# A re-annealed order of the steps of attention, routing and the first expert, under a list scheduler

## The chip, the cores and the metric

The kernel runs on one core of one Trainium2 chip. Times are device microseconds (us) of that core. A run is called fast or slow by the rules of the measurement; every run here counted as fast, but the mean granted TensorE clock of single runs still differs (0.994 to 1.000). The engines are PE (matmul; PEld is its weight load), DVE (vector), ACT (scalar), POOL (GpSimd) and SP (which issues transfers).

## The reference, cut to what matters

```python
def phi(x):                                   # attention features, of q and of k
    proj = einsum('bhsd,df->bhsf', x, w_phi)
    proj = proj - max(abs(proj), axis=-1)
    return concatenate([exp(proj), exp(-proj)], axis=-1)
# 8 batches, 8 heads, 576 rows, 64 columns; 128 features, twice
num, den = q_p @ (k_p.T @ v), q_p @ sum(k_p)  # x = num / den, as [4608, 512]
P = exp(x @ w_gate)                           # routing: 8 rounds of row and column scaling
for e in range(8):                            # eight experts, all of them on all rows
    out += P[:, e:e+1] * (relu(x @ w1[e]) @ w2[e])
```

The routing needs all of x (its column sums run over all 4608 rows). So attention has to end before the routing can start. The first expert's two products need no routing weights until they are scaled, so they serve as filling material for PE during attention and during the routing.

## The kernel before

The program is written as a list of small operations with a modelled duration each. A list scheduler turns the list into one fixed instruction order per engine:

```python
    def schedule(self):
        ...
            best = None
            for eng, rq in ready.items():
                ...
                for o in rq:
                    t = self.start(o, f)
                    if t is not None and (best is None or (t, o.idx) < best[:2]):
                        best = (t, o.idx, o)      # earliest start, then written order
        ...
            if o.nbytes:                          # a transfer: one server for all of them
                dma_free = max(at + o.dur + 1.0, dma_free) + o.nbytes / 1e3
                o.end = dma_free + 1.0
```

What is changed is the written order of the steps:

```python
    STEPS = {"a": stage_a, "q": lambda i: qs[i](), "r": stage_r, "b": stage_b,
             "c": lambda j: pair_c(j // 4, j % 4, xbs[j]), "g": stage_g,
             "u": lambda i: up0(i // 4, i % 4), "d": lambda i: down0(i // 4, i % 4)}
    order = ("aqraqabbcqabqacbqrbcaqbacuqaqbacqruabgqccucbudbduaqabdqadgrcbucqucabqcauqdua" ...)
    for i, n in enumerate(order):
        STEPS[n](order[:i].count(n))
    gate(8)
    ...
    routing()
    for i in fill:                                # the rest of the first expert
        expert0(i)
```

The letters: a takes a pair of heads (keys, scores, maxima, exponentials) and issues the loads of the next batch; q does the same for queries; r is the rest rows; b the products of attention; c the transposition into xT; g the logits; u and d are each one of 36 steps of the first expert's up and down product (8 matmuls of 512 columns in a step). A step a also issues a transposing transfer of what was loaded:

```python
            load_qk(b + 1, 2 * pr, 4, t, gt)      # POOL queue: two loads with a cast
            load_v(b + 1, 2 * pr, 4, t, gt)       # SP queue
            if b + 1 >= 2:
                turn_qk(t)                        # SP queue: dma_start_transpose, qkT<-qk
        ...
            load_w0(n, gt)                        # POOL queue: a piece of the first expert
```

After P exists, the first expert's results are scaled by it on ACT, while PE goes on with the second expert:

```python
        if e == 1 and g < 9:
            for ts in range(4):
                act(512, lambda ts=ts: nc.scalar.activation(
                    out=acc[g][:, ts, :], in_=acc[g][:, ts, :], func=ACT.Copy, bias=0.0,
                    scale=P[:, 4 * g + ts, 0:1]), ["P", ("acc", g, ts)] + akey(g), ...)
```

Of the kernel before, what the change touches and what calls it, by code (L numbers as in the profile page):

```python
# [168 lines left out]
def kernel(  # L169
# [636 lines left out]
    def stage_g(b):  # L806
# [5 lines left out]
             "c": lambda j: pair_c(j // 4, j % 4, xbs[j]), "g": stage_g,  # L812
             "u": lambda i: up0(i // 4, i % 4), "d": lambda i: down0(i // 4, i % 4)}
    order = (
        "aqraqabbcqabqacbqrbcaqbacuqaqbacqruabgqccucbudbduaqabdqadgrcbucqucabqcauqdua"
        "bgcbqaducdcqubcrbaudqauqdacbcdqduardqbbgcubuaqcaubgcdqacdqabubruqadbqadcbqbu"
        "cagcquaubqrdbadqaudbcqcaucbdcccqbgcg"
    )
    for i, n in enumerate(order):
        STEPS[n](order[:i].count(n))  # L820
# [456 lines left out]
```

## Time and profile before

| Kernel before | us |
|---|---|
| time, median of 3 runs | 1044.51 |
| span of the profiled run | 1043.5 |
| routing starts (attention is over) | 220.9 |
| P is written | 257.2 |
| PE alone carries the chain from | 298.2 |

The table of windows of the kernel before, three stretches of it. Columns: the stretch, its length, then busy us of each engine with the number of its instructions, the granted clock, the DMA share and GB/s.

```profile
core 0: us, PE busy (x) PEld busy (x) DVE busy (x) ACT busy (x) POOL busy (x), PEclk, DMA share, GB/s
50.00:75.00 25.00, 22.83 (x281) 15.07 (x280) 24.16 (x61) 24.00 (x66) 19.49 (x39) 1.00 1.32 196
75.00:100.00 25.00, 25.00 (x251) 15.63 (x251) 23.34 (x57) 23.84 (x62) 15.78 (x31) 1.00 0.89 156
225.00:250.00 25.00, 25.00 (x124) 12.09 (x123) 21.66 (x60) 10.35 (x18) 0.00 (x0) 1.00 0.49 179
```

In attention three engines are nearly full at once. In the routing (225 to 250 us) PE and DVE are, and ACT is not.

The two moments that divide the kernel, from the views of the two source lines: the routing's first reduce and the last instruction of P (duration in ns as smallest, median and largest, then the start in us of the first and the last such instruction).

```profile
L873 DVE TENSOR_REDUCE rr<-L x1: 444/444/444, 220.9 to 220.9; 128x36 f32<-128x288 f32 x1
L886 DVE TENSOR_TENSOR P<-T,c_bc x1: 457/457/457, 257.2 to 257.2; 128x288 f32<-128x288 f32 x1
```

The chain of work that ended last, in order of time (start, length, what):

```profile
218.43 38.47 PE P L407 x216
...
257.66 3.17 ACT acc L1181 x5
...
298.23 733.88 PE P L1019 x6720
```

PE fills the routing with first-expert matmuls (38.47 us), ACT's scalings follow P, and from 298 us on PE streams without a break.

Waits between 25 and 218 us, the ones of ACT and DVE for PE (who waited for whom, total us, times, longest):

```profile
DVE kv L587 <- PE P L407: 4.8, 5, 1.8
ACT hT L699 <- PE P L407: 3.7, 8, 1.2
ACT q L403 <- PE P L606: 3.6, 7, 0.8
DVE rec L624 <- PE P L611: 3.5, 9, 0.6
```

### The profile page before, as it was taken

How to read it: one execution, taken by the hardware profiler on the slowest of the kernel's cores; microseconds unless marked ns; L12 is line 12 of the kernel's file. 1: busy time of each engine (PE TensorE's matmuls, PEld its weight loads, DVE VectorE, ACT ScalarE, POOL GpSimd, SP SyncE). 2: the span in 40 equal slices, each digit the busy share in tenths (PEclk: the TensorE clock that was granted, in tenths of full speed). 3: DMA queues.
4: the chain of work that ended last, by engine and by line, in shares of the span. 5: the costliest groups of instructions: out<-in, count | busy, mean ns of one | idle time of the engine just before them, and what ended most of it. 6: DMA issues, size and time to landing. Idle time of an engine off the chain costs nothing.

```text
span 1043.5 us, 24529 instructions
## 1 busy us (share of the span) xinstructions
PE 1020.4 (98%) x9512; PEld 842.1 (81%) x9512; DVE 823.9 (79%) x1626; ACT 711.1 (68%) x1570; POOL 461.5 (44%) x532
## 2 busy tenths in 40 slices
PE   6899999999999999999999999999999999999998
PEld 4566666654788888888888888888888888888886
DVE  6999899998777787778877787778777877787775
ACT  7999999944976666666666666565666666666663
POOL 3876757500233344344444444444444443333442
PEclk9999999999999999999999999999999999999999
DMA  9997987734411152113311441134111611114333
GB/s 250 150 196 132 150 127 136 122 122 120 93 41 41 52 105 60 51 42 82 81 41 42 87 87 51 42 69 95 41 42 50 125 51 42 41 43 131 122 122 122
DMA packets 105237, 93.94 MB, mean 90 GB/s; under 512 B 45344, under 2 KB 80288, under 8 KB 105120
## 3 DMA queue, kind: packets, MB, share of 16 engines
q1 hardware_dynamic: 71840, 68.45, 23.6%
q0 software_dynamic: 33120, 23.86, 16.4%
q8 instruction: 74, 1.21, 0.5%
q14 instruction: 43, 0.35, 0.1%
q10 hardware_dynamic: 160, 0.07, 0.0%
HBM read 94.98 MB, written 14.16 MB: 105 GB/s over the span
## 4 chain that ended last, share of the span: by engine, by line
PE 89%; ACT 5%; DVE 3%; DMA 1%; issue 1%; SPq 0%; POOL 0%; DVEq 0%; ACTq 0%
PE P L1019 70%; PE P L407 16%; ACT acc L1181 2%; DVE m L399 1%; PE P L606 1%; ACT k L403 1%; DMA acc<-in_q_dram 1%; DMA wgate_f<-in_moe_w_gate_dram 1%; ACT V L1171 1%; ACT U L1047 1%; PE P L645 1%; DVE xb L626 0%; ACT q L403 0%; DVE P L618 0%; PE P L484 0%
## 5 line engine op out<-in xcount | busy, mean ns | idle before, releaser
L1174 POOL TENSOR_TENSOR acc<-acc,V 128x512 f32<-128x512 f32 x248 | 316.4, 1283 | 440.4 <-ACT V L1171 437.2
L1051 DVE CUSTOM_DVE_ANT_0 hT<-P,U 128x512 bf16<-128x512 f32 x378 | 255.0, 687 | 107.9 <-ACT U L1047 59.7
L1047 ACT COPY U<-P 128x512 f32<-128x512 f32 x378 | 217.8, 590 | 137.4 <-PE P L1019 130.8
L1171 ACT ACTIVATE V<-P,P 128x256 f32<-128x256 f32 x496 | 206.3, 477 | 123.4 <-PE P L1019 121.6
L1159 DVE SCALAR_TENSOR_TENSOR acc<-P,P,acc 128x256 f32<-128x256 f32 x372 | 160.1, 478 | 73.4 <-PE P L1019 71.7
L1019 PEld LDWEIGHTS <-w 128*128 128x128 bf16 x2016 | 197.3, 98 | 23.7 <-issue 0.6
L1019 PEld LDWEIGHTS <-S 128*128 128x128 bf16 x1984 | 194.1, 98 | 23.2 <-issue 0.6
L1019 PEld LDWEIGHTS <-T 128*128 128x128 bf16 x1512 | 147.9, 98 | 19.1 <-issue 2.0
L1019 PEld LDWEIGHTS <-hT 128*128 128x128 bf16 x1488 | 145.4, 98 | 18.3 <-DVE hT L1051 1.1
L1019 PE MATMUL P<-X,w 128*128 128x256 bf16 x1008 | 154.7, 273 | 0.4 <-ACT U L1047 0.4
L1019 PE MATMUL P<-xT,w 128*128 128x256 bf16 x1008 | 152.0, 273 | 0.0
L1019 PE MATMUL P<-X,T 128*128 128x256 bf16 x1008 | 148.6, 273 | 1.3 <-ACT U L1047 1.2
L1019 PE MATMUL P<-w,hT 128*128 128x256 bf16 x992 | 142.6, 273 | 0.6 <-DVE hT L1051 0.6
L1019 PE MATMUL P<-T,S 128*128 128x256 bf16 x1056 | 136.3, 273 | 0.4 <-ACT V L1171 0.4
L1019 PE MATMUL P<-w,S 128*128 128x256 bf16 x928 | 126.6, 273 | 0.0
L532 POOL TENSOR_TENSOR v<-v_m,em 128x512 bf16<-128x512 f32 x64 | 66.8, 1043 | 70.6 <-ACT em L403 57.5
L399 DVE TENSOR_REDUCE m<-P 128x4 f32<-128x512 f32 x128 | 82.7, 681 | 1.7 <-PE P L407 1.2
L1056 ACT ACTIVATE hT<-P 128x512 bf16<-128x512 f32 x126 | 74.6, 607 | 12.9 <-PE P L1019 12.4
L407 PE MATMUL P<-w,hT 128*128 128x512 bf16 x320 | 80.2, 379 | 0.3
L927 DVE TENSOR_TENSOR S<-hT 128x1024 bf16<-128x1024 bf16 x124 | 80.1, 683 | 0.0
L407 PE MATMUL P<-xT,w 128*128 128x512 bf16 x288 | 76.2, 379 | 1.2 <-ACT kr L403 0.5
L1019 PE MATMUL P<-xT,T 128*128 128x256 bf16 x504 | 76.3, 273 | 0.0
(94 smaller groups left out, 1091.7 us busy)
## 6 DMA issues: line engine op xcount, KB each, us to landing
X<-xd SPq DMA_DIRECT2D x126, 256.0 KB, 2.6
w<-in_moe_w_dram POOLq DMA_DIRECT2D x14, 1024.0 KB, 10.4
v_m<-in_v_dram SPq DMA_DIRECT2D x15, 512.0 KB, 5.1
out_dram<-acc SPq DMA_DIRECT2D x14, 512.0 KB, 3.2
xd<-S SPq DMA_DIRECT2D x18, 256.0 KB, 2.0
qk<-in_k_dram POOLq DMA_DIRECT2D x12, 256.0 KB, 5.5
qk<-in_q_dram POOLq DMA_DIRECT2D x12, 256.0 KB, 6.4
w<-in_moe_w_dram POOLq DMA_DIRECT2D x8, 256.0 KB, 7.5
```

Source lines behind the costliest of these rows:

```text
L399: dve(el, lambda: nc.vector.tensor_reduce(out=dst(), in_=src(), axis=AX.X, op=ALU.max, apply_absolute_value=True), r, w)
L407: nc.tensor.matmul(out_, lhsT=lhsT, rhs=rhs, start=start, stop=stop)
L532: pool(512, lambda y=y, em=em: nc.gpsimd.tensor_tensor(out=s["v"][y]()[:, :, 0:D], in0=t["v"]()[:, h0:h0 + 2].rearrange("p a (b c) -> p (a ...
L927: lambda: f.tensor_tensor(out=out_(), in0=x(), in1=y(), op=op), r, w, **kw)
L1019: pe(256, lambda i=i, k=k, z=z: nc.tensor.matmul(bank()[:, 256 * i:256 * i + 256], lhsT=lhs(k, i), rhs=rhs(k), start=first and z, stop=k = ...
L1047: act(512, lambda: nc.scalar.copy(out=u[fp][n]().rearrange("p a b -> p (a b)"), in_=x[fp]()), [x[fp]], [u[fp][n]])
L1051: dve(500, lambda: nc.vector._custom_dve(ADD_SAT, out=out_(fp, i, j), in0=bank[fp]().rearrange("p (a b) -> p a b", a=2), in1=u[fp][n](), s ...
L1056: act(512, lambda: nc.scalar.activation(out=out_(fp, i, j), in_=x[fp]().rearrange("p (a b) -> p a b", a=2), func=ACT.Relu, bias=0.0, scale ...
L1159: dve(330, lambda n=n, ts=ts: nc.vector.scalar_tensor_tensor(out=acc[g][:, ts, 256 * j:256 * j + 256], in0=bank()[:, 256 * n:256 * n + 256 ...
L1171: act(390, lambda n=n: nc.scalar.activation(out=u()[:, n, :], in_=bank()[:, 256 * n:256 * n + 256], func=ACT.Copy, bias=0.0, scale=P[:, 4 ...
L1174: pool(670, lambda: nc.gpsimd.tensor_tensor(out=acc[g][:, 2 * i:2 * i + 2, 256 * j:256 * j + 256], in0=acc[g][:, 2 * i:2 * i + 2, 256 * j: ...
L1181: act(512, lambda ts=ts: nc.scalar.activation(out=acc[g][:, ts, :], in_=acc[g][:, ts, :], func=ACT.Copy, bias=0.0, scale=P[:, 4 * g + ts, ...
```

## The change

Its intent: the written order is the priority of the list schedule. A search by annealing on the model of that schedule found another string with the same letters.

```diff
     order = (
-        "aqraqabbcqabqacbqrbcaqbacuqaqbacqruabgqccucbudbduaqabdqadgrcbucqucabqcauqdua"
-        "bgcbqaducdcqubcrbaudqauqdacbcdqduardqbbgcubuaqcaubgcdqacdqabubruqadbqadcbqbu"
-        "cagcquaubqrdbadqaudbcqcaucbdcccqbgcg"
+        "raqaqbabqacqaqbbrarccqbcabugucqabuqacqbcauqabbqcbadcruuuqbccaaqqbcbraddqugag"
+        "qbbdauqdbucaqrcccauaqbdccbuqgudabqadbdqdbcccrauqdaugdbcquaduqbaqcabudbcrqdaq"
+        "ccadbbuguqbadauuqcdbcuccaqudqbcbgcdg"
     )
```

## The prediction

> What bounds it now. (1) Attention, 0 to about 218 us. The table of windows gives, for 25 to 200 us (175 us), DVE 160 us busy, ACT 165, PE 167. No engine is the bottleneck alone: the waits from 25 to 218 us leave only 13.9 us idle on DVE and 12.8 us on ACT. [...] I count PE by issue steps in the trace (0.216 us for a 512-column matmul, 0.109 us for 256 columns, about 0.03 us for 65): an estimate of 186 us of PE stream in 218 us. About 32 us of PE time is empty, some 12 us of it in the first 25 us, where the chain of waits runs through the first loads (acc from q 6.7 us, w_gate 6.4 us). (2) Routing, 218.6 to 257.6 us: a DVE chain of eight iterations of about 5 us; PE is filled meanwhile with first-expert work (one piece of 38.5 us in the chain). (3) After P exists, ACT is full from 257.7 to 298 us (36 scalings of acc, 25.0 us, plus U, V, hT). From 298 us to the end PE streams at its rate (918 matmuls per 100 us); the change cannot touch that.
>
> What the change does. It permutes one string of 188 letters: 32 each of a, q, b, c, 24 u, 20 d, 8 r, 8 g in both. No instruction is added or removed; busy time per engine should be the same within 1 us. The string only sets priority among ready operations, the buffer turn, and the place of the gates on loads. The new string starts with r (whose loads land only at about 10 us, so the scheduler still starts with a), and holds the d steps back (7 instead of 11 after 108 letters, equal near the end).
>
> What it can gain. Only idle of the joint bottlenecks before 218 us. With 13 us idle on ACT and DVE, both waiting mostly for PE (hT 3.7, q 4.8, kv 4.8, rec 3.5 us), I expect a better order to recover 3 to 5 us, minus a loss because the model's durations are not the chip's. All of a shift of the end of attention should pass to the end: routing and the ACT stage start earlier by as much, and PE has about 5 us of slack in the ACT stage (an estimated 35 us of stream in 40 us) to take a backlog.
>
> Prediction: attention ends near 214.5 us, P near 254 us, the PE-bound stage starts near 294.5 us, and the total falls by 3.5 us to 1041.0 us; range 1035.5 to 1046.0. Faster by over 2%: 0.02 (21 us would need nearly all the early idle of every engine); within 2%: 0.96; slower by over 2%: 0.02.
>
> What would show it. Right: same instruction counts; the routing's first reduce and P earlier by 2 to 6 us; waits of ACT and DVE for PE between 25 and 218 us less by about as much; unchanged length of routing (37 us), ACT stage (40 us) and the stream after it (745 us). Wrong: attention's end earlier but routing longer, because more deferred first-expert work shares PE and DVE with it; or the ACT stage longer because PE comes with a backlog.
>
> What would make it wrong: a load gated later by the new place of a or q, so that a transpose starts late; turns of the eight PSUM buffers that the model orders otherwise than the chip; or an order fitted so closely to the model's durations that real ones break it, which could cost a few us.

## More of the kernel before

```profile
L407 PEld LDWEIGHTS <-w 128*128 128x128 bf16 x220 | 19.3, 98 | 14.6 <-issue 1.8 <-DVE xb L626 0.3
L407 PEld LDWEIGHTS <-hT 128*128 128x128 bf16 x168 | 15.0, 98 | 11.0 <-issue 0.7
...
L407 PEld LDWEIGHTS <-hT 128*128 128x128 bf16 x25 | 2.5, 98 | 2.9
```

Of the first expert's 576 matmuls, 388 are done when attention ends, and 25 are still owed when P exists.

## The result, and the profile after

| | before | after |
|---|---|---|
| time, median | 1044.92 us (4 runs) | 1046.20 us (4 runs, 1045.06 to 1047.42) |
| ratio | | 1.001 (95%: 0.9996 to 1.0024) |
| routing starts, profiled run | 220.9 | 219.6 |
| P begins, profiled run | 257.2 | 255.7 |
| span, profiled run | 1043.5 | 1045.1 |

Ratios are the mean time of one kernel's fast runs over that of the other's of the same rounds, so they are not quite the ratio of the medians quoted. The two kernels are equal within the measurement. The forecast gain of 3.5 us did not come. (The median of 1046.2 us is also 0.2 us above the top of the stated range; the ratio applied to the 1044.51 us of before gives 1045.6 us, inside it.)

The profile after, the same two lines:

```profile
L873 DVE TENSOR_REDUCE rr<-L x1: 447/447/447, 219.6 to 219.6; 128x36 f32<-128x288 f32 x1
L886 DVE TENSOR_TENSOR P<-T,c_bc x1: 459/459/459, 255.7 to 255.7; 128x288 f32<-128x288 f32 x1
```

P comes 1.5 us earlier, yet the span is 1.6 us longer. So something after P became 3.1 us longer, and something before it ate part of the gain. The first-expert weight loads, again up to the start of the routing and after P:

```profile
L407 PEld LDWEIGHTS <-w 128*128 128x128 bf16 x206 | 18.1, 98 | 12.3 <-issue 0.9
L407 PEld LDWEIGHTS <-hT 128*128 128x128 bf16 x167 | 14.9, 99 | 9.6 <-issue 0.5
...
L407 PEld LDWEIGHTS <-hT 128*128 128x128 bf16 x40 | 3.9, 98 | 4.7
L407 PEld LDWEIGHTS <-w 128*128 128x128 bf16 x1 | 0.1, 98 | 0.1
```

The new order has done 373 of the matmuls when attention ends, 15 fewer than the old one, and owes 41 when P exists, 16 more. At 0.216 us each (a run of eight takes 1.73 us in the chain of waits) that is 3.2 us of work not done in attention, and 3.5 us of work left for after P.

The chain that ended last, after:

```profile
61.10 14.54 DMA qkT<-qk
...
279.42 9.82 PE P L1019 x86
289.28 744.44 PE P L1019 x6817
```

Two things are new in it. From P to 279 us the chain still goes over ACT, but PE carries it from 279 us instead of 298: from there on PE is the late one now, not ACT. And there is a transposing transfer of 14.54 us. Around its landing the table of windows shows, after:

```profile
70.00:72.00 2.00, 2.00 (x22) 1.17 (x22) 1.70 (x5) 2.00 (x7) 1.66 (x5) 1.00 1.29 161
72.00:74.00 2.00, 0.66 (x19) 0.53 (x15) 1.54 (x6) 0.82 (x2) 0.00 (x0) 1.00 1.33 166
74.00:76.00 2.00, 0.31 (x3) 0.29 (x4) 0.00 (x0) 0.00 (x0) 0.00 (x0) 1.00 1.38 66
76.00:78.00 2.00, 1.78 (x18) 1.20 (x18) 1.44 (x3) 1.82 (x4) 1.56 (x2) 0.73 1.08 231
78.00:80.00 2.00, 2.00 (x17) 1.18 (x17) 1.63 (x4) 1.90 (x6) 0.00 (x0) 0.50 1.04 274
```

and before, for comparison, the third of these five stretches (PE is busy throughout all five there):

```profile
74.00:76.00 2.00, 2.00 (x14) 0.93 (x12) 2.00 (x6) 2.00 (x5) 0.40 (x2) 1.00 1.07 174
```

PE stands still from 72.7 us, all engines from 73.5 to 75.6 us. Then the granted clock falls to a half for some 3.4 us (it is 0.91 from 80 to 82 us). The lost clock is (0.27 + 0.50) x 2 = 1.5 us in the two rows shown. PE's own waits between 60 and 80 us name the reason:

```profile
PE P L407 <- DMA qkT<-qk: 3.0, 1, 3.0
```

The half clock follows the stall: here it comes after a wait of 3.0 us between matmuls. In the tables of windows of four later profiles, t_first (longest wait of PE around the stall 3.2 us; granted clock 0.55, 0.50, 0.50 and 0.74 in the four rows from 68 to 76 us) and early_rest_after (3.2 us; 0.70, 0.50 and 0.95 from 74 to 80 us) show the dip too, and after_again (0.8 us) and warm (2.0 us) stay at 1.00. From what length on a wait lowers the clock is not shown. A long wait is not the only way in: in the profile of hold1_before (below) the mean granted clock is 0.84 from 200 to 222 us, with PE busy for 17.45 of these 22 us, though its longest wait listed between 180 and 225 us is 0.8 us.

The waits that the prediction named did shrink: kv 4.8 to 3.2 us, hT 3.7 to 2.2, q 3.6 to 2.3, rec 3.5 to 3.0, together 4.9 us. But these four are a selection: over all waits of ACT and DVE for PE between 25 and 218 us the sum is 24.0 us in both profiles, because the stall brings new ones (ACT's `k` waits 4.6 us for PE instead of 1.5). In the profile of after_again (below), where PE waits only 0.8 us for the transposition, the sum is 19.1 us (25 to 214 us). So the new order does save waits, as it was made to, but only where the stall does not take them back.

### The profile page after: what moved, and what is told of

The parts are those of the page before. It is cut to its first block, busy times and chain, and to the rows that moved or that the text cites. A ratio compares the mean times of both kernels' runs of the same rounds, so it can differ in the third digit from the quotient of the medians.

```text
span 1045.1 us, 24505 instructions
## 1 busy us (share of the span) xinstructions
PE 1017.6 (97%) x9474; PEld 842.4 (81%) x9512; DVE 826.5 (79%) x1626; ACT 711.2 (68%) x1570; POOL 460.4 (44%) x532
## 4 chain that ended last, share of the span: by engine, by line
PE 91%; DMA 3%; DVE 2%; ACT 2%; issue 1%; SPq 0%; DVEq 0%; ACTq 0%
PE P L1019 72%; PE P L407 16%; DMA qkT<-qk 1%; PE P L606 1%; ACT acc L1181 1%; DVE m L399 1%; DMA acc<-in_k_dram 1%; DMA acc<-in_q_dram 1%; PE P L645 1%; DVE xb L626 0%; PE P L484 0%; ACT U L1047 0%; PE P L611 0%; SPq L329 0%; ACT acc L734 0%
## 5 line engine op out<-in xcount | busy, mean ns | idle before, releaser
L927 DVE TENSOR_TENSOR S<-hT 128x1024 bf16<-128x1024 bf16 x124 | 83.3, 709 | 0.0
L403 ACT ACTIVATE q<-P 128x512 bf16<-128x512 f32 x128 | 71.7, 629 | 4.0 <-PE P L606 2.7
```

The lines of the kernel that those rows point to most:

```text
L403: act(el, lambda: nc.scalar.activation(out=dst(), in_=src(), func=ACT.Exp, bias=0.0, scale=scale), r, w)
L927: lambda: f.tensor_tensor(out=out_(), in0=x(), in1=y(), op=op), r, w, **kw)
```

## The experiments

Two theories at the start. A: the gain of the new order is real and one stall, on the late transposition, eats it. B: the gain was never real; small waits everywhere eat it. The first group of runs led to a third, C: the order moves first-expert work from before P to after it, and the end pays for it. All experiments but hold1_before keep the fixed order of PE, ACT and DVE of the kernel that they start from; some repeat an instruction in it or add matmuls.

### The kernel after, once more, and its runs by clock

> The kernel after, unchanged, as the base of this group. Both theories: 1.000 to 1.002 of before. The four earlier runs fall in two groups by the mean granted clock: 0.997 to 0.998 with 1046.9 and 1047.4 us, 0.999 with 1045.1 and 1045.5 us. If the clock dip after the stall at 72.7 us comes and goes, these five runs show both groups again, about 1.7 us apart.

Six runs: 1043.79, 1048.08, 1044.43, 1043.81, 1048.22 and 1043.08 us, median 1044.12; ratio to before 1.0001 (0.9983 to 1.0018). With the four earlier ones there are ten. The four with a mean clock of 0.998 or less lie at 1046.88 to 1048.22 us (mean 1047.65), the six others at 1043.08 to 1045.51 us (mean 1044.28). So there are two groups, 3.4 us apart, which is more than the 1.7 us expected: it seems that the stall itself comes and goes, not only the clock. The profile of this kernel fell on a run without the dip (clock 1.000, 1043.79 us):

```profile
L873 DVE TENSOR_REDUCE rr<-L x1: 446/446/446, 216.4 to 216.4; 128x36 f32<-128x288 f32 x1
L886 DVE TENSOR_TENSOR P<-T,c_bc x1: 457/457/457, 252.5 to 252.5; 128x288 f32<-128x288 f32 x1
```

Undisturbed, the new order ends attention 4.5 us earlier than the old one, and P 4.7 us earlier: even more than I had forecast. But its span is 1042.0 us, only 1.5 us shorter. This is the main finding: 3.2 us are given back after P even where PE hardly stalls.

"Undisturbed" does not mean that the transposition was quick here. It took 14.3 us in this profile too, but it was issued at 59.4 us instead of 61.1, landed at 73.7, and PE waited 0.8 us for it instead of 3.0. The same DVE instructions of the two profiles start within 0.6 us of each other from 19 us until the stall. Right after it (`kv`, 74.6 against 76.6 us) the disturbed run is 1.9 us behind, at the end of the half clock (`rec`, 77.6 against 80.3 us) 2.8 us, and 3.1 us from 83 us on until the routing. In this pair of profiles, then, the stall makes about 1.9 us of the difference and the half clock 0.8 us.

### The transposition first

```diff
         done = self.schedule()
+        late = [done[n] for n in (844, 856, 877, 893)]   # k, q of the next half; two pieces of w2
+        for o in late:
+            done.remove(o)
+        n = done.index(self.ops[864]) + 1                # four POOL instructions later
+        done[n:n] = late
```

> The kernel after, with one thing moved: the four loads of GpSimd's queue (k and q of the next half batch, two pieces of w2) that start at 59.3 to 61.7 us, beside the transposing DMA of 61.1 us, are issued four GpSimd instructions later, so the transposition comes first. PE, ACT and DVE keep their order exactly. Theory A (the new order's gain is eaten by one stall: 3.0 us of all engines idle until the transposition lands at 75.6 us, then 1.7 us lost to a clock of a half): the transposition lands before 73 us, the stall shrinks under 1 us, no clock dip, and the time falls by 3 to 5 us against the kernel after, to 1041 to 1043 us. Theory B (the model's gain was never real; small waits all along the attention stage eat it): the stall shrinks, but the time stays within 1 us of the kernel after, because the work is late elsewhere.

The transposition landed after 6.7 us instead of 14.5, at 65.5 us. Yet the median was 1046.86 us, ratio 1.0019 (1.0006 to 1.0032). The profile shows why: the four issues now stood on POOL right in front of the rest rows' `vrd` work, each taking 0.7 to 0.8 us there, and PE waited for that instead.

```profile
PE P L412 <- POOL vrd L474: 3.9, 2, 3.2
```

The stall was replaced by another of the same size, with its own clock dip (0.50 in the two rows from 70 to 74 us). The run shows that the loads beside it lengthen the transposition (14.5 us with the four, 6.7 without). It says nothing about the time. The edit was careless: I had not looked at what POOL does next.

### PE kept busy through the stall

```diff
+    o = plan.ops[978]                     # the first matmul that reads the late tile
+    read, bank = o.fn, [b for b in o.bufs if b.ring.psum][0]
+    def filled():
+        for _ in range(14):
+            mm(bank()[:, 0:512], wphi2[:, 0, :], xT[:, 0, 0:512], True, True)
+        read()
+    o.fn = filled
```

> The kernel after, with 14 idle 512-column matmuls (14 x 0.216 us = 3.0 us) put on PE just before its first read of the late transposed tile, so PE works through the stall instead of resting; they write a bank that the next matmul overwrites, so the result is right. The stall of the other engines stays. Theory A with its clock part: the granted clock stays 1.00 from 75 to 85 us, mean clock 0.999 in every run, and the slow half of the runs disappears: 1045 us, that is 0 to 1.7 us under the kernel after of the same group. If the clock dip has another cause, the dip at 76 to 81 us stays.

Median 1046.64 us, ratio 1.0014 (1.0002 to 1.0026): no gain. In the profiled run the transposition landed even later (77.6 us), the other engines stood still for 4 us, and the clock stayed at 1.00:

```profile
74.00:76.00 2.00, 1.60 (x8) 0.51 (x6) 0.00 (x0) 0.00 (x0) 0.00 (x0) 1.00 1.19 33
76.00:78.00 2.00, 0.38 (x4) 0.35 (x5) 0.00 (x0) 0.00 (x0) 0.00 (x0) 1.00 1.73 111
78.00:80.00 2.00, 1.85 (x26) 1.35 (x24) 1.51 (x3) 1.89 (x4) 1.56 (x2) 1.00 0.86 188
```

So the filling keeps the clock up in this run. As a test of the time it was badly made: where the transposition is punctual, the 14 matmuls cost an estimated 3.0 us themselves (14 x 0.216 us), and two of its five runs still had a mean clock of 0.998. What the dip alone costs stays an estimate: 1.5 us of lost clock in the two rows above, of which 0.8 us reached DVE in the pair of profiles compared above.

### More work for one engine at a time, in the kernel before

In each kernel one instruction of the attention stage is repeated, with the same result, spread over 60 to 140 us.

```diff
+                    if 8 <= NP * b + pr < 19 and p0 == 1:      # more_pe: after the query matmul
+                        o = plan.ops[-1]
+                        o.fn = lambda once=o.fn: (once(), once(), once())
```

> The kernel before, with PE alone given more to do in the attention stage: the last 512-column matmul of the query step repeated twice in 11 steps (22 x 0.216 = 4.75 us, spread over some 60 to 140 us); the result is unchanged. If PE's stream up to the handover is what the total follows (my reading of the trace after, where P came 1.5 us earlier and the end 1.6 us later): the time rises by 3.5 to 4.8 us. If all three engines bind together, as the prediction had it: also 3 to 5 us. If PE has slack in this stage: under 2 us.

> The kernel before, with DVE alone given more to do in the same stretch: one reduce repeated in 8 steps (8 x 0.60 = 4.8 us). If the total follows PE alone: the time rises by under 2 us. If the engines bind together: 3 to 5 us.

> The kernel before, with ACT alone given more to do in the same stretch: one exp repeated in 10 steps (10 x 0.49 = 4.9 us). If the total follows PE alone: the time rises by under 2 us. If the engines bind together: 3 to 5 us.

| | added | time, median | ratio to before |
|---|---|---|---|
| before of this group | | 1044.34 | |
| more_pe | 4.75 us on PE | 1049.13 | 1.0040 (1.0023 to 1.0057) |
| more_dve | 4.8 us on DVE | 1048.36 | 1.0036 (1.0021 to 1.0051) |
| more_act | 4.9 us on ACT | 1047.90 | 1.0031 (1.0016 to 1.0045) |

Each engine's extra time passes to the end, by the ratios 4.2, 3.8 and 3.2 us of it. (The interval of more_act reaches down to 1.7 us; in its profile P starts 2.6 us later than before.) The attention stage is bound by three engines together, as the prediction had read it. "PE alone" is refuted for this stage. It also follows that 15 matmuls (3.2 us) that PE does not do in attention should make attention end some 3 us earlier: an estimate from more_pe, where 4.2 of 4.75 us passed. So, by this estimate, about 3 of the 4.5 us by which the undisturbed new order ends attention earlier are work postponed, not work saved.

### The rest rows' loads earlier

My next guess was that the four loads of the rest rows, which POOL issues in one burst at 42.0 to 44.3 us, start the lateness. The move is made by position in the list of scheduled operations, and only POOL's order changes:

```diff
-        done = self.schedule()
+        done = moved(self.schedule(), (536, 550, 570, 578), 217)    # behind the first w1 load
```

> The kernel after, with one thing moved: the four loads of k and q of the rest rows (batches 2 to 4), which start at 42.0 to 44.3 us just as the first transposing DMA (42.9 us) does, are issued right behind the first w1 load at about 21.6 us, where GpSimd has nothing to do until 28 us. PE, ACT and DVE keep their order. My theory now: PE's idle time before 300 us sets the end, and in the new order 5.6 us of it (even in a fast run without a clock dip; 0.9 us in the kernel before) lies between 60 and 130 us and comes from transposing DMAs that land 4 to 5 us later than the model put them, behind other loads. Then the first transposition lands near 47 us instead of 53, the second before 72 us instead of 73.7 to 77.6, PE idle between 60 and 130 us falls to 1 to 2 us, the runs with a low mean clock disappear, and the median falls to 1039.5 to 1041.5 us (0.995 to 0.998 of before). Rival: the idle time comes from the order itself (too little first-expert work at hand there); then the landings move but the idle time stays near 5 us and the time within 1 us of the kernel after.

> The same move in the kernel before (its four loads start at 40.7 to 47.6 us). There PE idles only 0.9 us between 60 and 130 us, so by my theory there is little to win: 0.998 to 1.001 of before. If it wins as much as in the kernel after, the order has nothing to do with it and the early loads help both alike.

Kernel after with it: median 1046.30 us, ratio 1.0009 (0.9995 to 1.0022), from 1043.43 to 1046.95 us. The first transposition landed at 49.4 us instead of 53.1, as expected, but the second still took 16.0 us and landed at 75.2 us. PE waited 3.2 us for it. Kernel before with it: 1045.74 us, ratio 1.0009 (0.9997 to 1.0022), no gain. So the burst at 42 us is not the cause of the second transposition's lateness: that half of the guess fell. And in the kernel before with the move the second transposition took 14.4 us instead of 10.6, though the next half's k and q loads kept their places (56.5 and 57.2 us), and PE waited 1.4 us for it. So the place of those two loads does not alone decide how long it takes; what else does stays open. In these five runs of the kernel after the mean clock did not sort fast from slow either (1046.95 us at 1.000, 1043.43 us at 0.997), so it is no reliable mark of the stall by itself.

### P later

```diff
                 out=cs(), in_=table(wv).transpose([0, 2, 1]), axis=AX.X, op=ALU.add), [wv], [cs])
+            o = plan.ops[-1]
+            o.fn = (lambda f=o.fn: (f(), f())) if it < 6 else o.fn
```

> The kernel after, with the routing's DVE chain made longer: the column reduce is repeated in six of the eight iterations (6 x 0.58 = 3.5 us; the result is unchanged), so the gate values P come 3 to 3.5 us later. My theory: in the new order PE still has some 9 us of first-expert work after P (P at 253.0, its last matmul at 262.0 us in the fast run), so P is not what the end waits for: the time rises by under 1 us. If every shift of P passes to the end, as the prediction said: plus 3 to 3.5 us.

> The same lengthening in the kernel before, where P came at 257.6 and PE's last first-expert matmul at 263.0 us, and where the chain of waits runs through ACT's scalings of acc from P to 298 us: here P has little slack, so plus 1.5 to 3.5 us by my theory, and plus 3 to 3.5 us if every shift of P passes to the end.

This failed as a test of its size: the stretch from the routing's first reduce to P grew by only 1.2 us in the kernel after (253.9 - 216.6 = 37.3 against 36.1 us) and 0.9 us in the kernel before, probably because DVE had gaps for most of the 3.5 us (it is busy for 21.66 of 25 us in the table above). The times were 1046.64 us (ratio 1.0027) and 1046.10 us (ratio 1.0019). My expectation that P has slack in the new order is not borne out. In both profiles the time from P to the end kept its length to 0.1 us, so this shift of P did pass to the end. In the fixed order PE's later matmuls stand behind the small ones of the routing (in the kernel before, two of these start at 229.56 us between first-expert matmuls, the next two at 234.88).

### One down step held back, in the kernel before

```diff
-        py = down(W[0][1], hts[g], tss, akey(g))
+        py = down(W[0][1], hts[g], tss, akey(g) + [("L", 8)] * (19 <= 4 * g + part < 20))
...
-        STEPS[n](order[:i].count(n))
-    gate(8)
+        n == "d" and order[:i].count(n) >= 19 or STEPS[n](order[:i].count(n))
+    gate(8); [down0(j // 4, j % 4) for j in range(19, 20)]
```

This one lets the scheduler make a new order. It is meant to isolate theory C: attention and P should stay where they are, and only the debt of first-expert work at P grows.

> The kernel before with one first-expert down step (the last d of the string) held until attention is over. Its hidden-layer buffers then stay taken, and the later first-expert steps queue up behind it: by the schedule's count 59 first-expert matmuls instead of 24 are left when P comes, while attention, routing and P keep their times. My theory (what PE still owes when P comes is paid in full at the end): P within 1 us of before, P to the end longer by 6 to 7.6 us (35 x 0.216 = 7.6), total 1050.5 to 1052 us. If the end follows P, and PE has 5 us of slack in the ACT stage to take a backlog (the prediction's claim): total up by 2.6 us at most.

Time 1053.31 us, ratio 1.0080 (1.0066 to 1.0094). The profiled run (span 1050.3 us):

```profile
L886 DVE TENSOR_TENSOR P<-T,c_bc x1: 458/458/458, 256.5 to 256.5; 128x288 f32<-128x288 f32 x1
```

and its first-expert weight loads after P:

```profile
L407 PEld LDWEIGHTS <-hT 128*128 128x128 bf16 x48 | 4.7, 98 | 5.7
L407 PEld LDWEIGHTS <-w 128*128 128x128 bf16 x12 | 1.2, 98 | 1.4
```

P is 0.7 us earlier than in the kernel before, and the end is 6.8 us later. From P to the end it takes 1050.3 - 256.5 = 793.8 us instead of 786.3: 7.5 us more, for 35 more matmuls owed (60 instead of 25), which at 0.216 us are 7.6 us. The debt is paid in full. (Its runs have a mean clock of 0.994 to 0.996; in the profiled one the dip lies at 200 to 222 us, before P, so it is not in this stretch.) The total is 1.3 us above my range, and attention, which should have stayed, ended 1.7 us earlier (219.2 us).

PE's first matmul of the second expert shows where the debt is paid, in the kernels before and after and in this one:

```profile
263.21 0.60 PE L1019 MATMUL P<-xT,w 128*128 128x256 bf16 x4
265.31 0.60 PE L1019 MATMUL P<-xT,w 128*128 128x256 bf16 x4
270.07 0.60 PE L1019 MATMUL P<-xT,w 128*128 128x256 bf16 x4
```

Counted from the start of P that is 6.0, 9.6 and 13.6 us: PE starts the second expert later by 3.6 and 7.6 us, and at the end it is still 3.1 and 7.5 us behind. PE does idle in the 50 us after P, for 2.8, 2.5 and 2.8 us, but in waits for the second expert's own U, V and hT, which a larger debt does not fill. The prediction's 5 us of slack on PE in the ACT stage do not exist as room for a backlog.

### The time from P to the end, over all runs

The span minus the start of P, from the two views of each profiled run:

| Order | first-expert matmuls owed at P | from P to the end, us | profiled kernels |
|---|---|---|---|
| old | 25 | 786.3 to 786.6 | before, more_pe, more_dve, more_act, early_rest_before, late_p_before |
| new | 41 | 789.4 to 789.5 | after, after_again, t_first, warm, early_rest_after, late_p_after, gap_after |
| old, one d held | 60 | 793.8 | hold1_before |

Within one order this last part is rigid. P itself moved by 6.2 us among the first six, and by 5.1 us among the next seven, and the rest followed unchanged. Between the orders it differs by 3.1 us, for 16 matmuls more (3.5 us).

### The loads in a gap of POOL

The last kernel puts the theories' two useful findings together: loads beside the transposition make it late (14.5 against 6.7 us in t_first), and POOL must not be kept from `vrd` (PE waited 3.2 us for it there). POOL idles for 2.2 us before its work at 57.1 us, so the next half batch's loads go there, 4.7 us earlier than they were; the rest rows' loads go where early_rest_after had them.

```diff
-        done = self.schedule()
+        done = moved(moved(self.schedule(), (512, 513, 515, 516), 219), (865, 866), 780)
```

> The kernel after with two moves on GpSimd's queue alone: the rest rows' loads at about 21.6 us as in early_rest_after, and the k and q loads of the next half batch (59.3 and 60.2 us) put into GpSimd's idle gap at about 54.7 us, so that the second transposing DMA no longer starts beside them; nothing is put in front of GpSimd's vrd work, which is what spoiled t_first. PE, ACT and DVE keep their order. My theory (the transposition is late because loads start beside it): it lands before 72 us, PE idle between 60 and 130 us falls from 5.6 to 7.4 us to 1 to 3 us, no run with a dipped clock, P at 249 to 251 us, P to the end stays 789 us, and the median is 1039.5 to 1041.5 us (0.995 to 0.997 of before). Rival (lateness is only one of many small waits of the order): 0.998 to 1.001 of before.

Median 1042.60 us (1042.20 to 1044.19), ratio to before 0.9983 (0.9970 to 0.9997), and no run with a mean clock under 0.999. The transposition landed at 72.1 us, 12.3 us after its issue, and PE no longer waits for it:

```profile
72.00:74.00 2.00, 2.00 (x34) 1.67 (x33) 2.00 (x8) 1.85 (x5) 1.32 (x2) 1.00 1.32 200
74.00:76.00 2.00, 1.63 (x19) 1.03 (x19) 2.00 (x4) 2.00 (x6) 0.22 (x1) 1.00 1.32 92
```

Attention ends at 215.2 us and P begins at 251.3 us. This kernel is faster than the kernel before by 0.17%, and by its median faster than every group of the kernel after. It stays 1 to 3 us short of my expectation; P and the landing miss theirs by 0.3 and 0.1 us. By the table of windows PE idles 4.6 us between 60 and 130 us, not the 1 to 3 us expected (7.4 and 5.6 us in the two profiles of the kernel after, 0.9 in the kernel before). PE's waits between 40 and 130 us are now many small ones for DVE (1.8 us for the maxima is the largest sum), so theory B keeps a part. Which of the two moves did it was not separated; early_rest_after alone did nothing.

## Why the prediction was right or wrong

- **No work is added or removed: right.** DVE, ACT, POOL and PEld have the same instruction counts in both profiles (1626, 1570, 532, 9512). DVE's busy time rose by 2.6 us, more than the 1 us allowed.
- **Three engines bind attention together: right.** more_pe, more_dve and more_act each passed to the end.
- **The order recovers 3 to 5 us of waits: right in what it saw, wrong in what it took it for.** In the undisturbed run all waits of ACT and DVE for PE fell from 24.0 to 19.1 us, and attention ended 4.5 us earlier (216.4 against 220.9). The forecast was 3.5 us: its 214.5 us counts from the 218 us at which PE begins to fill, not from the first reduce. In the disturbed run the four named waits shrank, their total did not. But 15 first-expert matmuls, some 3 us, were not saved. They were left for later.
- **"All of a shift of the end of attention should pass to the end ... and PE has about 5 us of slack in the ACT stage": this is the step that failed.** A shift of P passes in full only within one order. Between the two orders the part after P grew by 3.1 us, because PE owes 41 matmuls there instead of 25. The reading that ACT is full from 257.7 to 298 us and PE therefore has slack took a full engine for the only full one. hold1_before measured the slack: of 7.6 us of debt, 7.5 us were paid.
- **I counted letters and missed the debt.** I saw the d steps held back (7 instead of 11 after 108 letters) and wrote "equal near the end". The letters were equal in number. What the scheduler made of them was not: 373 against 388 matmuls at the handover. The statement named the possibility under what would show it wrong ("the ACT stage longer because PE comes with a backlog"), and that is what happened.
- **"A load gated later ..., so that a transpose starts late" was another named danger, and it came in part of the runs.** The transposition started at about the same time (61.1 against 60.8 us) but landed at 75.6 instead of 71.4 us. Two loads that the old order issues at 56.5 and 57.3 us start beside it at 59.3 and 60.2 us in the new one. It cost 3.0 us of standstill of PE, then some 3.4 us of a half clock. t_first (6.7 us with the four loads moved away) shows that loads beside it lengthen it, and gap_after (12.3 us with two of them moved) points the same way; but early_rest_before (14.4 us with the old places of the two) says that they are not the whole cause. In one pair of profiles the stall makes 1.9 us and the half clock 0.8 us; for the 3.4 us between the two groups of runs the shares stay open.
- **The sum.** Undisturbed: -4.7 us at P, +3.2 us after it, so 1.5 us gained, by one profile (the six such runs have a mean of 1044.28 us, 0.6 to 0.8 us under the medians of before, 1044.92 and 1045.03). Disturbed: -1.5 us at P, +3.1 us after it, so 1.6 us lost. The runs fall in both kinds, and the medians are equal within the measurement. That the total stayed within 2%, as forecast, is no success of the mechanism: the two terms that cancelled the gain were named as dangers and then left out of the sum.

Why did the annealing take this order? The kernel's own model, evaluated on the host for both strings after the prediction, gives 1044.6 and 1039.3 us. It has attention ending at 223.5 and 216.5 us, and the transposition landing at 71.3 and 71.2 us. The second values are near the undisturbed chip (216.4 us). But the first is 2.6 us worse than the chip's 220.9, and the model did not know the late landing (75.6 us). It also lets the part after P grow by only 1.6 us, where the chip shows 3.1. The search had an easy opponent in the model's picture of the old order.

## What to carry to other kernels

When a reordering moves a milestone forward, count what was done by then: an earlier milestone with less work behind it is a postponement, and the time from there to the end shows it. Before calling an engine's rest "slack", measure it by giving that engine a known debt. And an order that a search found on a model is as good as the model's least certain duration; here that was the landing of a transposing transfer, 14.5 us after its issue beside other loads and 6.7 us with four of them moved away.

## What the runs show of transfers and their issue

- The same transposing transfer took 6.7 us from issue to landing with the four loads moved away (t_first), 10.6 us in the kernel before (but 14.4 us in early_rest_before, with the old places of k and q), 12.3 us in gap_after, and beside all four 14.5 us (after), 14.3 (after_again), 16.0 (early_rest_after) and 17.8 (warm). PE waited for it for 3.0 us in the kernel after, 0.8 in after_again, 3.2 in early_rest_after, and not at all in gap_after.
- An issue costs the engine that makes it: 0.7 to 0.8 us on POOL for each of the four loads in t_first. That is little beside the transfer (in the kernel before up to 220 us a median of 5.5 and 6.4 us from the issue of a k or q load to its landing), but in t_first the four took 3.0 us of POOL in front of work on the critical path, and PE waited 3.2 us for it.
